# Linear attention and a gated FFN on one core: the seven-product projection starts one chunk earlier

## The chip, the core and the metric

The kernel is one program on one core of a Trainium2 chip. The metric is device time in microseconds; lower is better. The core has five instruction streams: TensorE (PE in the profile, with its weight loads as PEld), VectorE (DVE), ScalarE (ACT), GpSimd (POOL) and SyncE (SP), which here only issues transfers.

## The reference

Inputs are q, k and v of shape 8 x 8 x 576 x 64 (batch, heads, sequence, head width), two 512 x 1536 weights and one 1536 x 512 weight, all fp32.

```python
q_s = softmax(q, axis=-1)              # over the 64 features of a head
k_s = softmax(k, axis=2)               # over the 576 positions
kv  = einsum('bhsd,bhse->bhde', k_s, v)
x   = einsum('bhsd,bhde->bhse', q_s, kv)   # then laid out as 4608 tokens x 512
out = ((x @ w_a) * (x @ w_b)) @ w_out      # "gate", then "projection"
```

## The kernel before, in words

**Tiling.** The 4608 tokens are worked in nine chunks of 512, numbered c = 0 to 8. The 1536 hidden features are six pairs n = 0 to 5 of 256. Every matrix product is made at nearly fp32 accuracy out of three products of split numbers: each operand is kept as a rounded high part and the rest (`split`, L593: a copy on ACT gives the high part, a subtraction on DVE at L599 the low part), and high by high, high by low and low by high are added up in PSUM.

**Gate.** Chunk 0 takes the gate products plainly, while the weights are still being converted (the startup). From chunk 1 on each pair of x @ w_a and x @ w_b is a 2 x 2 block product made with seven block products in place of eight (L1127, 84 matmuls of 256 columns for a pair, 504 for a chunk). The seven x operands of the next chunk, B11, T2, T3, T1, B21, T4 and B22, are made at the end of a chunk by `x_operands` (L1055); four of them need subtractions, 128 x 512 each (L1071, L1072, L1077, L1082). These run on DVE, or on POOL when `lean` is set, which it is from the chunk before `SEVEN` on. The seven weight operands of a pair, 512 KB each, are read anew from memory for every chunk (`get_w`, L728 to L730), into eight buffers `ws`, or seven from chunk `SEVEN - 1` on (`few`, L1914).

**Projection.** Up to chunk `SEVEN - 1` it is the plain product (`project`, L1147): 12 feature blocks by 4 token blocks by 3 split products by 2 halves of 256 columns, 288 matmuls for a chunk (L1017, `po`). From chunk `SEVEN` on (4 before) it is made of seven block products too (`seven`, L1832): two halves by six pairs by 7 products by 3, 252 matmuls of the same 256 columns (L1847, `pp`). It needs more operands. The weight side is made once, pair by pair, in `seven_operands` (L1768): six instructions on POOL (L1774, L1779) and four splits for each of six pairs, at the places of the list `seven_places` (L1889): two pairs in chunk `SEVEN - 1`, four in chunk `SEVEN`, put into tiles that nothing uses any more by then. The activation side is made in `prepare` (L1790) for each half of each pair: four subtractions on POOL (L1817) and two splits. Its inputs are the gated features, whose four multiplications per pair are shared by DVE and POOL (`quarter`, L2002) from chunk `SEVEN` on, and are all on DVE before (L2022 to L2040, tile `cc`). `bring_out` (L1856) adds up the seven products of a half, four instructions on DVE and one on ACT, where the plain form has a copy on ACT.

**Attention.** The x of chunk c + 1 is worked out while chunk c multiplies (`attention_tasks`, L1250), from `SEVEN` on in another form. Keys up to there go through `key_steps` (L1178): maxima with three DVE instructions for each of four head groups, a reduction over the partitions on POOL (L767), a subtraction on DVE (L799). Later keys go through `keys_late` (L1201): a transposed copy of the keys is loaded (`ktt`), DVE takes the maximum of each row (L1212), TensorE transposes it (L949), it goes out to memory and back to all partitions (`dk`, `mk`), and POOL subtracts (L1234). The query addition (`q_exp`, L993) is on DVE before `SEVEN` and on POOL from it on (both L994). Chunk 3 has buffers of its own (`roomy`, L963).

**Order.** The order of work is written out: `ORDER` holds, for PE, DVE, ACT, POOL and SP, the list of all instructions by name, one step after the other, and `arrange` (L1655) chains each engine's instructions in that order. An item such as `pair.11*12` stands for the next 12 gate matmuls of step 11, where step numbers are 6(c - 1) + n; `proj`, `step` and `attend` are projection, the rest of a step, and attention. Each engine works through its list in that order, and what stands behind a waiting instruction waits too. The lists interleave gate, projection and attention matmuls closely, so that one product's wait is covered by another's matmuls.

```python
SEVEN = 4
(nc.gpsimd if c >= SEVEN else nc.vector).tensor_tensor(out=qt, in0=qt, in1=rows[0], op=ALU.add)
run_pending() if pend else seven()
```

Of the kernel before, what the change touches and what calls it, by code (L numbers as in the profile page):

```python
# [31 lines left out]
        "tr0*5 warm*25 tr1*5 pq0*4 pk0*10 pk1*10 tr3*4 tr2:4 pq1*4 tr3 tr2*4 px0 pk3*9 px1 pk3 pk2*10 pq2*4 "  # L32
        "pq3*4 g00*2 g00:10*8 g00*6 g00:4*4 px3 px2 g10:12*4 g10*20 g00*4 g01:12*3 g01*19 g11:12*4 g11*16 "
        "g01*2 g11*4 g20*12 g21*12 p0:2*2 p0*6 g20*12 g21*12 turn.0*3 proj.1:4 turn.0*2 proj.1:4 proj.1*2 "
        "proj.2*2 gate.3*48 proj.2:2*2 proj.1 proj.1:1 proj.1*2 proj.2:2*2 prod.0*10 gate.4*6 gate.4:18*24 "
        "proj.3:12*2 turn.1*4 proj.3:16*2 gate.4*18 proj.3*4 proj.3:12*2 proj.3:8*2 gate.5*12 proj.2*2 turn.1 "
        "gate.5:12*4 gate.5*2 proj.3:10*2 proj.3:2*6 gate.5:10*12 gate.5*6 gate.5:4*8 gate.5*3 proj.3:2*2 "
        "gate.5 turn.2*3 prod.1*10 turn.2 proj.4:6*2 proj.4:16*2 gate.6*11 gate.6:13*9 proj.3*2 proj.4*2 "
        "gate.6:13*3 gate.6*18 turn.3*4 gate.6*7 proj.4*8 proj.4:6*2 proj.4*8 proj.5:18*2 proj.5:12 "
        "proj.5:6*2 prod.2 turn.4*3 gate.7*10 proj.5:10*2 gate.7:14*4 proj.5:10 gate.7:14*2 proj.5 gate.7*2 "  # L40
        "proj.5*2 gate.7:12*4 prod.2 turn.4 gate.7:12*2 proj.5:9*4 proj.5 gate.7:12 gate.7*5 gate.7:7 "
        "proj.5:6*2 gate.7*2 proj.5:2*2 proj.5*2 turn.3 gate.7*3 gate.7:2*5 gate.7*5 proj.6*2 proj.6:16*2 "
        "proj.5*2 proj.6:4*2 proj.6:8*2 turn.5*4 prod.3*10 gate.7 proj.6:12*2 proj.6*2 proj.6:2*2 gate.7 "
        "proj.6*2 proj.6:2*6 gate.8*20 gate.8:4*7 proj.6*2 gate.8:4*7 gate.8*12 proj.7:12*2 proj.7:6*2 "
        "proj.7*2 proj.7:8*2 gate.8*2 proj.7:10*4 prod.4*2 turn.6*4 proj.7:8*2 proj.7:4*4 proj.7*4 turn.5 "
        "gate.9*11 gate.9:13*20 prod.5*10 proj.7*2 proj.8:18*2 proj.8*2 gate.9*13 proj.8:10*2 proj.8*2 "
        "proj.8:12*2 gate.9*4 proj.8:8*2 turn.7*3 gate.10*10 turn.7 prod.6*2 gate.10:14*12 proj.8:10*2 "
        "proj.8:2*2 gate.10*2 proj.8:2*2 proj.8:4*2 proj.8:2*2 gate.10:12*4 gate.10*8 gate.10:4*8 turn.8 "
        "gate.10*4 prod.7*2 proj.8*2 proj.9:6*2 proj.9*2 proj.9:8*2 proj.9*2 proj.9:10*2 prod.8 proj.9:2*2 "
        "proj.9:8*2 gate.11*15 gate.11:9*12 gate.11*9 proj.9:4*2 gate.11*4 proj.9:2*2 gate.11*4 proj.9*4 "  # L50
        "pair.0*9 proj.10*2 proj.9*2 gate.11*4 proj.10:10 proj.10:4*2 proj.10:8 pair.0 pair.0:14*6 pair.0*2 "
        "pair.0:12*2 pair.0*4 attend.0*10 pair.0:8 pair.0*9 proj.10:12*2 proj.10*2 pair.0 pair.0:13*3 "
        "proj.10:6*2 pair.0:13*3 proj.10:8*2 pair.0:13*3 pair.0:1*4 pair.0:9 pair.0:1*3 pair.0:6 pair.0:1*4 "
        "pair.0:2 pair.0 proj.10:6*2 pair.0 proj.0:12*2 proj.10*4 proj.0*2 proj.10*2 proj.0:4*4 proj.10*2 "
        "proj.0:10*4 pair.0:12*8 proj.0:10*2 pair.0*4 pair.0:8*4 pair.1 pair.0 proj.0*4 proj.0:2*2 pair.0 "
        "pair.1 pair.0 pair.1*3 proj.0:2*2 pair.0*5 proj.0*2 pair.1 pair.1:18*2 pair.1*5 pair.1:1 pair.1*5 "
        "pair.1:7*4 pair.1 attend.1 pair.1:6*2 pair.1*4 pair.1:2 pair.1:17*5 proj.1*2 pair.1*2 proj.1*2 "
        "pair.1*2 proj.1:14*2 pair.1:13*2 proj.1:2*2 pair.1 proj.1:12*2 pair.1:12*3 pair.1*10 proj.1:12 "
        "pair.1 proj.1:12 proj.1:2*2 pair.1:1 pair.1*2 proj.1:2*2 pair.1:12*5 proj.1:26*2 pair.1:12*5 "
        "proj.1:2*2 pair.1*4 attend.1 pair.1:8*2 pair.1*6 proj.1:12*2 proj.1:22*2 pair.2*4 proj.1:2*2 pair.1 "  # L60
        "pair.2 proj.1:10*2 pair.1 proj.1:18*2 pair.2 proj.1*2 proj.1:2*2 proj.1*2 pair.2:18*3 pair.2 "
        "pair.2:17*2 pair.2 pair.2:4*2 proj.1:6*2 attend.1 pair.2:14*3 pair.2*2 pair.2:2*3 pair.2:9 pair.2:2 "
        "pair.2 proj.1*2 pair.2:1 pair.2*3 proj.1:4*2 pair.2 proj.1:4*2 proj.1:2*2 pair.2*2 proj.1*2 "
        "proj.2:6*2 proj.2*2 proj.2:14*4 pair.2:3*4 pair.2 proj.2*2 pair.2:2*3 proj.2:2*2 pair.2:7*7 "
        "pair.2:2*4 pair.2*2 pair.2:1*4 pair.2 proj.2*2 pair.2 proj.2:10*2 attend.1*10 pair.2:12*5 pair.2*3 "
        "pair.2:9 pair.2*3 pair.2:6*2 pair.2*6 proj.2:8*2 proj.2:2*2 pair.2*2 proj.2:22*2 pair.2*2 proj.2:2*2 "
        "proj.2*2 proj.2:6*2 pair.3:12*2 pair.3*7 attend.1 pair.3 proj.2*2 proj.2:14*2 pair.3*3 proj.2*2 "
        "pair.3 proj.2:12*2 pair.3*4 pair.3:6*2 proj.3:18*4 pair.3:6 pair.3*3 pair.3:3*2 proj.2:6*4 pair.3*3 "
        "proj.3:18*2 pair.3 proj.2:6*2 proj.2*2 proj.3:12*2 pair.3:18*4 pair.3:6*3 pair.3 proj.2*2 attend.1 "
        "pair.3:14*3 pair.3:5 pair.3:13 proj.2*2 pair.3:13*2 attend.1 pair.3:13 pair.3 pair.3:4 pair.3 "  # L70
        "pair.3:3*2 proj.3:34*2 pair.3:3 pair.3 proj.3:12*2 proj.3:6*2 pair.3:2 proj.3:10*2 pair.3*2 "
        "attend.1*10 pair.3 pair.3:2 proj.3:28*2 proj.3*2 pair.3*2 proj.3:4*4 proj.3*2 pair.3:12*7 proj.3*2 "
        "pair.3:12*3 pair.3 pair.4 pair.3*2 pair.4 pair.3*2 pair.3:7 proj.3:6*2 pair.3:7 pair.4*2 proj.3:6*2 "
        "attend.2 pair.3 proj.3*2 pair.4 pair.3*3 proj.3*2 proj.3:4*2 pair.4 pair.3*3 pair.4:18*2 proj.3:8*2 "
        "proj.3*4 pair.4:18 pair.4*2 pair.4:4*4 pair.4*2 pair.4:10 pair.4 attend.2*10 pair.4:1*3 pair.4 "
        "pair.4:5*2 pair.4*2 pair.4:3 pair.4*2 proj.3*2 proj.4*2 proj.4:16*2 pair.4 proj.4*2 pair.4*2 "
        "proj.4:2*2 proj.3*2 proj.4:12*2 proj.4:6*2 pair.4 proj.4:6*2 pair.4 proj.4:2*2 pair.4:1 pair.4*3 "
        "attend.3 pair.4*2 proj.4*2 attend.3*2 proj.4*2 pair.4 pair.4:6*2 pair.4*4 attend.3 pair.4 attend.3 "
        "pair.4:1*6 proj.4:2*2 pair.4 pair.4:16*2 pair.4*2 attend.3 proj.4:20*2 proj.4*2 pair.4 pair.4:13*3 "
        "pair.4 pair.4:12*2 proj.4:12*2 proj.4:6*2 pair.4:12*3 proj.4:14*2 pair.4*7 proj.4:10*2 pair.4 "  # L80
        "proj.4*2 pair.4*3 pair.4:1*2 pair.5*2 attend.4 pair.5*2 pair.4 proj.4*2 pair.5 attend.4*3 pair.5:19 "
        "pair.5 pair.5:18*2 pair.5 attend.4 proj.4:2*2 pair.5:5 proj.4*2 pair.5 pair.5:4 pair.5*3 attend.4 "
        "pair.5:11 proj.4:2*2 pair.5:1 proj.4*2 pair.5:10 pair.5:1*2 pair.5:8 proj.5:6*4 pair.5:1 proj.4*2 "
        "pair.5:7 pair.5*2 proj.5:8*2 pair.5 pair.5:4 proj.5:6*2 pair.5:4 pair.5 pair.5:3 proj.5:10*2 "
        "proj.5*2 pair.5*2 proj.5*2 attend.4 pair.5 pair.5:14*2 attend.4 pair.5*2 attend.4*2 pair.5:12*3 "
        "attend.4*2 pair.5*5 proj.5:2*2 pair.5:7*2 proj.5:14*2 pair.5 proj.5:4*2 pair.5:6 pair.5*3 proj.5*2 "
        "pair.5*2 proj.5:2*2 pair.5*5 proj.5*2 proj.5:6*2 proj.5:8*2 pair.5*6 proj.5:8*2 pair.5 pair.6 "
        "proj.5:10*4 pair.5*2 attend.4 pair.5 pair.6 pair.5 proj.5*2 pair.6*2 pair.5 attend.4*2 proj.5*4 "
        "attend.4*2 pair.6 attend.4 pair.6 proj.5*2 pair.5*8 proj.6:6*2 pair.5*4 pair.6*4 proj.5:2*2 "
        "proj.6:16*2 pair.6:2 pair.6 proj.6*2 proj.6:14*2 pair.6 proj.6:4*2 pair.6*7 proj.5*2 proj.6:6*2 "  # L90
        "pair.6 proj.6:4*2 pair.6 pair.6:2 pair.6*2 proj.6:4*2 pair.6:23 proj.6:6*2 pair.6:23*3 proj.6:12*2 "
        "proj.6*2 proj.6:2*2 pair.6*8 pair.6:15 proj.6*2 pair.6 pair.6:2*3 pair.6:11*2 pair.6:2*2 pair.6*3 "
        "pair.6:6 proj.6:10*2 pair.6*2 proj.6:6*2 pair.6*4 pair.6:16 proj.6:12*2 pair.6 proj.6:8*2 "
        "proj.6:10*2 proj.6:6*2 proj.6*2 pair.6*3 pair.6:12*3 pair.6*5 pair.6:7*3 proj.6:6*2 pair.6 pair.7*2 "
        "pair.6*2 pair.7*2 pair.6*2 pair.6:2 pair.7 pair.6:2*2 pair.6 pair.6:1 proj.6*2 pair.7 proj.6:2*2 "
        "pair.6:1 pair.6 attend.6*20 pair.7 pair.7:5 pair.7 proj.6*2 pair.7:4*3 pair.7*2 pair.7:2*3 pair.7 "
# [2005 lines left out]
```

## Time and profile before

| what | value |
|---|---|
| time, median of 3 runs | 947.04 us (946.09 to 949.88) |
| time of the profiled execution | 951.79 us |
| its span, first to last instruction | 949.8 us |
| TensorE busy in it | 904.1 us, 95% |
| DVE, ACT, POOL busy | 688.7, 423.0, 383.6 us |
| transfers | 259.26 MB, mean 273 GB/s |

The profiled execution is one run; 2.0 us of its time lie outside the span. The kernel's source lines are those of the listing above. Helpers record many operations under one line (L599 is every low part of a split, L1127 every gate matmul), so the tile written and read tells them apart: `gl<-cc` is the split of the gated features, `xo<-xf` that of an x operand, `ws<-dw` a weight read.

Chunks do not show in the profile by name. Their borders are found by counting along TensorE's list in `ORDER`, since its matmuls run in that order: the first gate matmul of chunks 1 to 6 starts at 143.1, 251.6, 362.8, 466.1, 551.3 and 649.6 us, that of chunk 7 at 748.7 us.

### The profile page before, as it was taken

To read this page: it belongs to the slowest core of one execution; us is meant where nothing else is said; L and a number is where in the kernel's file an instruction comes from. 1 tells how busy PE (TensorE), PEld (TensorE's weight loads), DVE (VectorE), ACT (ScalarE), POOL (GpSimd) and SP (SyncE) were. 2 spreads that over 40 slices of the span, in tenths; PEclk is the share of its full clock that TensorE was granted. 3 is DMA by queue.
4 is the path that set the end of the run, shared out by engine and by line. 5 is a ranking of instruction groups with operands and counts; after the bars stand their busy time and mean duration, and the time that the engine had idled before them with its cause. 6 is when DMAs were issued, how large, how long until landed. Compare 5 with 4: busy or idle time off the path is not lost.

```text
span 949.8 us, 21010 instructions
## 1 busy us (share of the span) xinstructions
PE 904.1 (95%) x7973; PEld 880.3 (93%) x7973; DVE 688.7 (73%) x1197; ACT 423.0 (45%) x1170; POOL 383.6 (40%) x464
## 2 busy tenths in 40 slices
PE   7999987999999989999999999999999999999997
PEld 6888987999999989998989999999999999999997
DVE  7999898887875486755877596768666756774555
ACT  8877874533552233522553346234532452332122
POOL 1554443232010070413285465463635633662434
PEclk9999999999999999999999999999999999999999
DMA  9787957998999974999599988995999289838851
GB/s 345 299 312 271 374 209 262 324 321 271 299 338 275 304 261 146 321 285 311 184 307 328 330 294 308 312 336 176 328 285 342 93 300 288 315 104 278 273 167 45
DMA packets 93027, 259.26 MB, mean 273 GB/s; under 512 B 11184, under 2 KB 13312, under 8 KB 92928
## 3 DMA queue, kind: packets, MB, share of 16 engines
q1 hardware_dynamic: 92928, 257.94, 80.6%
q8 instruction: 63, 1.03, 0.5%
q14 instruction: 36, 0.29, 0.1%
HBM read 218.86 MB, written 36.94 MB: 269 GB/s over the span
## 4 chain that ended last, share of the span: by engine, by line
PE 58%; DVE 19%; DMA 12%; issue 4%; ACT 3%; POOL 3%; SPq 1%; DVEq 0%; POOLq 0%; ACTq 0%
PE pp L1847 11%; PE kp L1127 11%; PE ka L1127 9%; PE kx L1127 9%; PE po L1017 8%; DMA ws<-dw 6%; PE ky L1127 5%; DVE gl L599 3%; DVE xo L599 2%; DMA dw<-ws 2%; PE pk L837 2%; DVE room_wy L630 2%; DMA mr<-dq 1%; PE px L1045 1%; DVE ws L599 1%
## 5 line engine op out<-in xcount | busy, mean ns | idle before, releaser
L1127 PE MATMUL ka<-xo,ws 128*128 128x256 f32 x1152 | 169.7, 280 | 7.6 <-DVE xo L599 2.3
L1127 PE MATMUL kx<-xo,ws 128*128 128x256 f32 x1152 | 170.8, 279 | 1.7 <-DVE xo L599 1.0
L1127 PE MATMUL kp<-xo,ws 128*128 128x256 f32 x1152 | 165.2, 280 | 7.2 <-DVE u L1980 3.9
L1127 PEld LDWEIGHTS ka<-xo,ws 128*128 128x128 f32 x1152 | 148.9, 189 | 9.3 <-DVE xo L599 2.5
L1127 PEld LDWEIGHTS kp<-xo,ws 128*128 128x128 f32 x1152 | 146.6, 188 | 9.9 <-DVE u L1980 5.0
L1127 PEld LDWEIGHTS kx<-xo,ws 128*128 128x128 f32 x1152 | 149.6, 188 | 2.6 <-DVE xo L599 1.2
L1017 PE MATMUL po<-wo_w,gh 128*128 128x256 f32 x720 | 121.1, 279 | 0.0
L1017 PEld LDWEIGHTS po<-wo_w,gh 128*128 128x128 f32 x720 | 100.6, 189 | 0.2
L1127 PE MATMUL ky<-xo,ws 128*128 128x256 f32 x576 | 84.3, 280 | 3.7 <-DMA ws<-dw 3.1
L930 ACT ACTIVATE qt<-qt,st 128x64 f32<-128x64 f32 x224 | 75.6, 340 | 24.9 <-DVE st L927 24.9
L1017 PE MATMUL pt<-xo,ws 128*128 128x256 f32 x576 | 77.4, 284 | 5.8 <-DVE ws L599 2.3
L1127 PEld LDWEIGHTS ky<-xo,ws 128*128 128x128 f32 x576 | 74.4, 189 | 4.8 <-DVE qtt L994 1.4
L1017 PEld LDWEIGHTS pt<-xo,ws 128*128 128x128 f32 x576 | 70.4, 188 | 9.1 <-DVE ws L599 2.8
L1847 PE MATMUL pp<-wo_w,gh 128*128 128x256 f32 x392 | 73.4, 279 | 0.3 <-ACT gh L596 0.2
L1017 PE MATMUL po<-wo_w,gl 128*128 128x256 f32 x360 | 68.7, 283 | 2.0 <-DVE gl L599 2.0
L748 POOL TENSOR_TENSOR room_wy<-room_wy 128x512 f32<-128x512 f32 x24 | 34.0, 1421 | 68.2 <-DMA room_wy<-dy 57.3
L1817 POOL TENSOR_TENSOR s<-room_wy 128x128 f32<-128x128 f32 x64 | 35.0, 550 | 64.2 <-DVE gl L599 37.5
L1847 PEld LDWEIGHTS pp<-wo_w,gh 128*128 128x128 f32 x392 | 58.9, 188 | 0.7 <-ACT gh L596 0.7
L627 POOL TENSOR_TENSOR room_wr<-raw,room_wr 128x512 int32<-128x512 int32 x24 | 36.3, 1517 | 56.0 <-DVE raw L624 40.2
L1980 DVE TENSOR_TENSOR u<-ky,u 128x512 f32<-128x512 f32 x48 | 32.9, 685 | 35.2 <-PE ky L1127 20.9
L1847 PE MATMUL pp<-wt,gh 128*128 128x256 f32 x294 | 56.2, 281 | 0.5 <-ACT gh L596 0.5
L1017 PEld LDWEIGHTS po<-wo_w,gl 128*128 128x128 f32 x360 | 53.7, 190 | 3.1 <-DVE gl L599 2.6
(216 smaller groups left out, 1907.5 us busy)
## 6 DMA issues: line engine op xcount, KB each, us to landing
ws<-dw SPq DMA_DIRECT2D x260, 512.0 KB, 6.4
dw<-ws SPq DMA_DIRECT2D x42, 512.0 KB, 6.3
raw<-in_w_ab SPq DMA_DIRECT2D x24, 512.0 KB, 7.9
mr<-dq SPq DMA_DIRECT2D x96, 128.0 KB, 6.8
out<-room_wr SPq DMA_DIRECT2D x36, 256.0 KB, 5.5
vt<-in_v SPq DMA_DIRECT2D x28, 325.0 KB, 5.2
qt<-in_q SPq DMA_DIRECT2D x32, 256.0 KB, 5.3
kt<-in_k SPq DMA_DIRECT2D x24, 320.0 KB, 5.2
```

The lines of the kernel that those rows point to most:

```text
L599: return nc.vector.tensor_tensor(out=lo, in0=src, in1=hi.bitcast(F32), op=ALU.subtract)
L627: nc.gpsimd.tensor_tensor(out=r, in0=u, in1=r, op=ALU.add)
L630: nc.vector.scalar_tensor_tensor(out=yi, in0=yi, scalar=-(2 ** 31), in1=r, op0=ALU.bitwise_and, op1=ALU.bitwise_or)
L748: nc.gpsimd.tensor_tensor(out=a[o], in0=a[x], in1=a[y], op=op)
L837: nc.tensor.matmul(pk[h * D:(h + 1) * D], kt[:, j, h], vt[:, j, h], start=(j == 0), stop=(j == J - 1),)
L930: nc.scalar.activation(out=qt[:, j, h], in_=qt[:, j, h], func=AF.Exp, bias=st[:, h, 0, j:j + 1], accum_out=st[:, h, 1, j:j + 1],)
L1017: ins = nc.tensor.matmul(out[:, n * H:(n + 1) * H], w, x[:, n * H:(n + 1) * H], start=start and n == 0, stop=stop, skip_group_check=True,)
L1045: nc.tensor.matmul(px[:, s], w, m[:, s], start=(i == 0), stop=(i == 2))
L1127: ins = nc.tensor.matmul(pt[:, n], w[:, n, wp, c], x[:, xp, c], start=(first and n == 0 and i == 0), stop=(i == 5), skip_group_check=True,)
L1817: nc.gpsimd.tensor_tensor(out=t[:, o], in0=a, in1=b, op=op)
L1847: nc.tensor.matmul(pp[bank][:, place], parts[x][:, o], w[b][y], start=(n == 0 and place == 0 and k == 0), stop=(n == NI - 1 and k == 2), s ...
L1980: nc.vector.tensor_tensor(out=u2, in0=ky, in1=u2, op=ALU.add)
```

## The change

`SEVEN` goes from 4 to 3. With it move: chunk 3's projection (seven block products, not the plain form), the two and four sets of weight operands (chunks 2 and 3, not 3 and 4), `lean` x operands for chunk 3, the seven instead of eight `ws` buffers in chunk 2, the POOL form of chunk 3's query addition, `keys_late` for the keys that chunk 3 brings in (batch 3), and chunk 3's gated features in the shared form. `roomy` holds for no chunk any more. Since odd chunks take the pairs in falling order, the list of places now goes by position and not by pair number. The input holds transposed keys from batch 3 on.

All five lists are new from the first instruction on: the startup and every other chunk, too, run in another order. Their lengths, in instructions:

| engine | before | after |
|---|---|---|
| PE | 7588 | 7553 |
| DVE | 1197 | 1186 |
| ACT | 897 | 907 |
| POOL | 456 | 524 |
| SP | 702 | 710 |

```diff
 ORDER = {
     "PE": (
...
@@ -507,7 +489,7 @@
     NCH = NT // T
     LATE = NCH - qt_late.shape[0]
     ODD = 16
-    SEVEN = 4
+    SEVEN = 3
 
     const = ctx.enter_context(tc.tile_pool(name="const", bufs=1))
@@ -1886,13 +1868,14 @@
+    p = pairs_of(SEVEN)
     seven_places = [
         (SEVEN - 1, 1, lambda: homes("mr.0") + homes("mr.1")),
         (SEVEN - 1, 2, lambda: odd_homes("ws.7") + one_home("xt.0") + one_home("xt.1")),
-        (SEVEN, 0, lambda: [room("cc.0", n) for n in range(3)] + b12_home(2)),
-        (SEVEN, 0, lambda: [room("cc.0", 3)] + [room("xo.8", n) for n in range(2)] + b12_home(3)),
-        (SEVEN, 1, lambda: [room("xo.9", n) for n in range(2)] + [room("xo.10", 0)] + b12_home(4)),
-        (SEVEN, 1, lambda: [room("xo.10", 1)] + b12_home(0) + b12_home(1) + b12_home(5)),
+        (SEVEN, 0, lambda: [room("cc.0", n) for n in range(3)] + b12_home(p[2])),
+        (SEVEN, 0, lambda: [room("cc.0", 3)] + [room("xo.8", n) for n in range(2)] + b12_home(p[3])),
+        (SEVEN, 1, lambda: [room("xo.9", n) for n in range(2)] + [room("xo.10", 0)] + b12_home(p[4])),
+        (SEVEN, 1, lambda: [room("xo.10", 1)] + b12_home(p[0]) + b12_home(p[1]) + b12_home(p[5])),
     ]
@@ -1972,7 +1955,7 @@
             for m, (at_c, at_n, places) in enumerate(seven_places):
                 if (c, n) == (at_c, at_n):
-                    seven_operands(m, places(), m % 2 * 4 * T if c < SEVEN else 4 * T)
+                    seven_operands(p[m], places(), m % 2 * 4 * T if c < SEVEN else 4 * T)
@@ -2069,7 +2052,7 @@
-    klate = k[4:].reshape(b - 4, g, 2, s, d).transpose(0, 1, 2, 4, 3).reshape(b - 4, g, P, s)
+    klate = k[3:].reshape(b - 3, g, 2, s, d).transpose(0, 1, 2, 4, 3).reshape(b - 3, g, P, s)
```

In the new POOL list the first two sets of weight operands (`step.7`, `step.8`) stand right behind the last weight sums of chunk 1 (`step.4`), three of their instructions even before the last of them; in the list of before (`step.13`, `step.14`) they stand behind the partition reductions of chunk 2 (`attend.7`).

794 rows, old and new, of the table ORDER are left out of this document.

## The prediction

> **What bounds the kernel now.** I read the page first (busy times and the chain), then the busy times by chunk, then what TensorE waited for, then the stretch with the longest wait.
>
> The page: span, busy time by engine, and the chain that ended last.
>
> ```profile
> span 949.8 us, 21010 instructions
> PE 904.1 (95%) x7973; PEld 880.3 (93%) x7973; DVE 688.7 (73%) x1197; ACT 423.0 (45%) x1170; POOL 383.6 (40%) x464
> ...
> PE 58%; DVE 19%; DMA 12%; issue 4%; ACT 3%; POOL 3%; SPq 1%; DVEq 0%; POOLq 0%; ACTq 0%
> ```
>
> TensorE sets the time, but a third of the chain runs over others, so the order counts. Busy time by stretch (length; busy time and instructions for PE, PEld, DVE, ACT, POOL; granted clock; DMA share and GB/s): the startup, chunks 1 to 6, a dense stretch of chunk 8, then four short ones.
>
> ```profile
> 0.00:143.10 143.10, 129.02 (x1095) 119.24 (x1095) 129.65 (x217) 113.60 (x277) 58.78 (x47) 1.00 0.81 300
> 143.10:251.60 108.50, 99.74 (x874) 96.70 (x875) 90.18 (x165) 44.04 (x118) 30.79 (x22) 0.98 0.87 292
> 251.60:362.80 111.20, 104.54 (x927) 102.40 (x926) 76.44 (x142) 40.84 (x123) 20.54 (x18) 0.98 0.88 283
> 362.80:466.10 103.30, 99.71 (x912) 97.87 (x911) 68.75 (x126) 39.27 (x122) 24.19 (x18) 1.00 0.83 271
> 466.10:551.30 85.20, 82.68 (x754) 80.79 (x753) 60.73 (x106) 39.22 (x118) 49.84 (x57) 1.00 0.93 311
> 551.30:649.60 98.30, 96.68 (x876) 95.14 (x875) 72.34 (x124) 40.97 (x122) 54.90 (x76) 1.00 0.86 288
> 649.60:748.70 99.10, 96.00 (x865) 94.05 (x865) 66.72 (x119) 38.53 (x118) 52.46 (x74) 1.00 0.82 269
> 850.00:900.00 50.00, 50.00 (x439) 49.96 (x438) 27.77 (x46) 10.41 (x23) 19.57 (x39) 1.00 0.79 264
> 237.00:252.00 15.00, 15.00 (x130) 15.00 (x129) 12.53 (x24) 5.50 (x11) 1.38 (x1) 1.00 0.84 258
> 343.00:358.00 15.00, 11.48 (x94) 11.08 (x93) 14.13 (x16) 6.26 (x15) 9.62 (x8) 0.99 0.59 200
> 449.00:464.00 15.00, 14.32 (x121) 13.72 (x120) 14.10 (x22) 5.72 (x16) 4.01 (x3) 1.00 0.66 227
> 357.60:361.01 3.41, 3.41 (x18) 3.41 (x18) 2.47 (x6) 0.00 (x0) 0.00 (x0) 0.50 0.00 0
> ```
>
> Length less PE's busy time is its idle time: 14.1 us in the startup, then 8.8, 6.7, 3.6, 2.5, 1.6 and 3.1 in chunks 1 to 6. In the dense stretch there is none, and 439 matmuls less about two that began before it give 50 / 437 = 114 ns a matmul. Chunk 2 has the most idle time of the chunks that the change rewrites, over half of it at its end, 343 to 358 us, where PE idles 3.5 us and DVE is busy for 14.13 of 15. There, on PE, DVE and POOL (start, length, what; in brackets the idle time before it):
>
> ```profile
> 350.06 0.74 PE L1017 MATMUL po<-wo_w,gl 128*128 128x256 f32 x4 [1.16 <-DVE gl L599]
> ...
> 356.50 0.74 PE L1127 MATMUL kp<-xo,ws 128*128 128x256 f32 x4 [2.36 <-DVE u L1980]
> ```
>
> ```profile
> 344.83 0.68 DVE L2039 TENSOR_TENSOR cc<-ka,u 128x512 f32<-128x512 f32 x1
> 345.43 1.41 DVE L1072 TENSOR_TENSOR xt<-xf,xt 128x512 f32<-128x512 f32 x1
> 346.25 4.34 POOL L1779 TENSOR_TENSOR room_wy<-room_wy 128x256 f32<-128x256 f32 x4
> 348.80 2.35 DVE L599 TENSOR_TENSOR gl<-cc,gh 128x512 fp32r<-128x512 f32 x2
> ```
>
> The end of chunk 2 does two jobs at once: DVE makes chunk 3's x operands, subtractions and splits, while POOL makes the first weight operands of the projection. DVE instructions with two inputs in SBUF take up to twice the 0.68 us that one reading PSUM takes. Two results that PE needs come late, and then the granted clock is 0.50 for 3.41 us, in which 18 matmuls start where 3.41 / 0.114 = 30 would: 12 x 0.114 = 1.4 us lost.
>
> **The change part by part.** The sum is made against the profiled execution's own 951.79 us (span 949.8 and 2.0 around it), 4.75 above the median of 947.04; I take the difference off the median.
>
> *Matmuls.* Chunk 3's projection falls from 288 to 252, all of 256 columns: 36 x 0.114 = **-4.1 us**. PE is busy for 96 to 98% of these chunks, so I count all of it (bounds -4.1 and, if the time saved all turned into waiting, 0).
>
> *Keys and queries of chunk 3.* Rows of the groups involved, in their forms before and after (mean ns behind the busy time):
>
> ```profile
> L949 PE MATMUL pst<-ident,st 128*4 128x128 f32 x4 | 1.1, 270 | 0.0
> L767 POOL PARTITION_ALL_REDUCE mx<-m x4 | 3.6, 922 | 40.5 <-DVE m L778 40.5
> L799 DVE TENSOR_TENSOR kt<-kt,mx 128x640 f32<-128x640 f32 x4 | 3.2, 814 | 0.0
> L994 POOL TENSOR_TENSOR qtt<-qtt,mr 128x512 f32<-128x512 f32 x20 | 27.8, 1390 | 57.6 <-DMA mr<-dq 39.4 <-DVE xf L1296 10.6 <-DMA qtt<-in_q_late 4.0
> L1234 POOL TENSOR_TENSOR kt<-kt,mk 128x640 f32<-128x640 f32 x16 | 25.7, 1613 | 42.9 <-DMA ws<-dw 29.7 <-DMA kt<-in_k 9.5 <-PE ky L1127 1.8
> L1212 DVE TENSOR_REDUCE st<-ktt 128x1 f32<-128x576 f32 x16 | 11.6, 741 | 0.0
> ```
>
> PE gets one transposition (**+0.1**; at most its whole 0.27). Four partition reductions leave POOL (3.6 us), and eight additions come, 4 x 1.39 + 4 x 1.61 = 12 us, beside 111 us in which POOL works 20.5. DVE loses the subtractions (3.2 us) and gets four reductions (3.0). Neither is on PE's path unless late; a wait of POOL for `mk` delays the x of chunk 3 alone, needed a chunk later.
>
> *Chunk 3's projection inputs.* 60 more POOL instructions (12 multiplications, 48 subtractions) make chunk 3 like chunk 4 is now: POOL 49.8 us instead of 24.2, in 85 us. Chunk 4 idles 2.5 us and chunk 3 3.6, chunk 5 1.6 and chunk 4 2.5: if each takes on the row of the next, **-2.0** over both; I take half, **-1.0**, since the keys differ (bounds -2.0 and +2).
>
> *The end of chunk 2.* The four x subtractions move to POOL and the weight operands are already made: what chunk 3's end is now, where the same lean form idles 15 - 14.32 = 0.7 us in its 15 us against 3.5. I take **-2.4**, leaving 0.4 for a second small wait (bounds -3.5 and 0). Without a wait of this length there is no half clock: **-1.4** (bounds -1.4 and 0).
>
> *Two sets of weight operands at the end of chunk 1.* 12 POOL instructions and eight splits now stand where DVE makes chunk 2's x operands, in the 15 us around 237 to 252, where PE now never idles and DVE has 2.5 us to spare. The nearest row for the same collision is the 3.5 us at the end of chunk 2. I take **+2.0** (bounds 0 and 3.5, and 1.4 more if the clock falls too), between the two because DVE has more room here.
>
> The Trainium skill has a rule that speaks against this: GPSIMD Engine Reference, Key points, says that GpSimd shares its SBUF interfaces with VectorE and contends with DVE instructions that have two SBUF inputs. The trace agrees: the 1.41 and 2 x 1.18 us above, under POOL's 4.34. It makes the moved collision one of the rivals.
>
> *Transfers.* Chunk 2 gets four transposed key blocks and the maxima's round trip, and one weight buffer fewer.
>
> ```profile
> ktt<-in_k_late SPq DMA_DIRECT2D x4, 288.0 KB, 9.4
> room_wy<-dq SPq DMA_DIRECT2D x16, 128.0 KB, 7.8
> ```
>
> 4 x 0.295 + 0.26 (two blocks like the second row's) = 1.4 MB at chunk 2's 283 GB/s, 5 us of transfer time. SP issues eight more, queued among the weight reads that PE needs. Chunk 2's DMA share is 0.88, so it fits; I take **+1.0** (bounds 0 and 5).
>
> *The lists.* Every engine's order is new. Chunks 5 and 6 do the same work and idle 1.6 and 3.1 us: a spread of 1.5 for a chunk, over nine stretches 1.5 x 3 = 4.5. One chunk that came out as chunk 1 does now instead of as chunk 5 would cost 8.8 - 1.6 = 7. I take **0**, bounds -4.5 and +7.
>
> Sum: -4.1 + 0.1 - 1.0 - 2.4 - 1.4 + 2.0 + 1.0 = -5.8, about -6: 946 for a run like the profiled one, **941 us** at the median.
>
> **The rivals.**
>
> *The collision only moves.* The wait at the end of chunk 2 comes back at the end of chunk 1, whole, and with the half clock: 3.5 + 1.4 for 2.0, +2.9 on the sum, 944 us. For it: the new POOL list puts the weight operands there. Against it: DVE's 2.5 us to spare, and PE's 15.00.
>
> On the clock, the Trainium skill (TensorE: Matmul & The Clock Gate, Why this matters for your kernels) says no idle gap over about 3 us. Here 1.16 and 2.36 us within 8 us were enough, so by the trace the 1.4 us would come with the moved wait; by the rule they would not, and this rival would be at 943 in place of 944.
>
> *Transfers run out (the other side).* Chunk 3 shrinks by up to 18 us, from 103.3 to chunk 4's 85.2, with its transfers unchanged. DMA-busy time now is 0.88 x 111.2 + 0.83 x 103.3 = 183.6 us in chunks 2 and 3; with 5 more 188.6, in 111 - 5 + 85 = 191: a share of 0.985. The long stretches above reach 0.93 at most. At 0.93 the two chunks take 203, 12 us more than forecast: 953 us. Slower than now from a share of 188.6 / 197 = 0.96 down. Against it: the seven buffers of 512 KB are 3.7 MB, 12 us at 311 GB/s, that can be read ahead, and chunk 4 at 0.93 idles only 2.5 us.
>
> *The lists decide.* Startup and chunk 1, which hold 22.9 us of idle time and nothing of the change, come out 4.5 us better or 7 us worse: 936.5 or 948.
>
> That the change does not do what it says I leave out: the list of PE is 35 shorter.
>
> **How the numbers follow.** Forecast 0.50, moved collision 0.24, transfers 0.12, lists better 0.07 and worse 0.07. A difference of 0.5% (4.7 us) is about what a measurement tells from none: faster is below 942.3, slower above 951.8. Faster: 0.43 of the forecast's 0.50 (its own range is 937 to 945), 0.05 of the collision, 0.07 of the lists: 0.55. Slower: 0.10 of the transfers, 0.01 of the collision and 0.01 of the worse lists: 0.12. Same: the rest, 0.33. The range is 934 (all bounds of gain at the end of chunk 2 with better lists) to 950 (worse lists, or transfers at a share of 0.945); beyond it lie the worst 0.10 of the transfers and some 0.05 at the fast end.
>
> **What would show it.** PE matmuls fall by 35 and L1017 `po` by 288, L1847 `pp` grows by 252. At the end of chunk 2 no PE wait above 1 us, and granted clock 1.00 there. At the end of chunk 1 a PE wait on a DVE split or `u`, with POOL L1779 above it: under 2 us for the forecast, 3.5 for the rival. DMA share in chunk 3 of 0.95 or more with PE waits on `ws<-dw` under 2 us in all; above 5, the transfers decide. PE idle of startup and chunk 1 within 4.5 of 22.9. The forecast is wrong if the time stays above 945 or if the gain comes from the startup.

## The result and the profile after

| | before | after |
|---|---|---|
| time, median of 4 runs each on one chip | 946.57 us (945.44 to 949.88) | **903.93 us** (899.82 to 905.43) |
| ratio, 95% interval | | **0.954** (0.950 to 0.958) |
| span of the profiled execution | 949.8 us | 901.9 us |

The change made the kernel 42.6 us faster. The forecast was 941 us, a gain of 6, and its range ended at 934: the sign was right, the size wrong by a factor of seven. The two profiled executions lie 47.9 us apart, because the one of before was 5 us above its median; numbers by stretch contain these 5 us, and those of other kernels a like difference where their profiled run is off the median.

Lines up to about L1870 stand 18 lower in the kernel after: the gate matmuls are L1109, the low part of a split is L581, the plain projection L999, the one of seven products L1829.

The page of the kernel after: span, busy time by engine, and the chain that ended last.

```profile
span 901.9 us, 21088 instructions
PE 882.2 (98%) x7938; PEld 868.1 (96%) x7938; DVE 655.1 (73%) x1186; ACT 426.4 (47%) x1180; POOL 428.1 (47%) x532
...
PE 89%; DMA 5%; DVE 2%; POOL 2%; issue 1%; ACT 1%; SPq 0%; POOLq 0%; DVEq 0%; ACTq 0%
```

The chain tells most: PE's share of it goes from 58% to 89%, and DVE's from 19% to 2%. The span splits in three. PE's idle time falls from 949.8 - 904.1 = 45.7 us to 901.9 - 882.2 = 19.7, by 26.0. The 35 matmuls fewer give 35 x 0.114 = 4.0. But PE's *busy* time falls by 21.9, 17.9 more than these 35 explain: the same matmuls are recorded as shorter. The ends of matmuls are modelled, and a matmul whose successor comes a little late fills the time between; at most 2.8 of it were the two half clocks of before (1.4 us each). So some 15 us of what the old profile shows as busy was not work of the matmuls. The starts bear this out: time over 114 ns from one matmul's start to the next's, where the profile counts no idle time, adds up to 54.5 us before and 36.2 after, 18.2 less. That these were short waits for operands is the likely reading; no run shows it one by one. The Trainium skill says this of the view I used (Perfetto Trace Analysis, Identifying the Most-Contended Engine): busy time of pipelined matmuls is no good measure of how near TensorE is to its limit. The 17.9 us agree that it is none, though the reason given there, that pipelined instructions look smaller, is another.

Busy times by stretch of the kernel after: the startup, chunks 1 to 8, then the ends of chunks 1 and 2 (columns as in the prediction; borders counted along PE's new list).

```profile
0.00:136.00 136.00, 126.65 (x1101) 119.88 (x1102) 115.76 (x220) 113.50 (x280) 62.47 (x48) 1.00 0.89 326
136.00:234.70 98.70, 98.14 (x897) 96.87 (x895) 84.31 (x167) 46.06 (x125) 37.77 (x28) 1.00 0.96 331
234.70:337.60 102.90, 99.42 (x911) 97.69 (x910) 77.09 (x136) 47.07 (x155) 30.19 (x25) 1.00 0.89 302
337.60:421.30 83.70, 82.61 (x768) 81.45 (x768) 61.78 (x110) 36.01 (x102) 52.24 (x61) 1.00 0.95 323
421.30:513.30 92.00, 92.00 (x846) 90.99 (x845) 64.35 (x118) 40.04 (x120) 51.59 (x72) 1.00 0.90 300
513.30:609.60 96.30, 95.99 (x884) 95.22 (x883) 69.93 (x125) 42.49 (x126) 54.06 (x76) 1.00 0.92 300
609.60:704.10 94.50, 94.50 (x863) 93.56 (x862) 66.83 (x120) 44.26 (x149) 49.18 (x70) 1.00 0.82 274
704.10:793.60 89.50, 89.50 (x785) 89.50 (x784) 55.93 (x95) 29.28 (x70) 46.38 (x73) 1.00 0.79 254
793.60:901.90 108.30, 103.37 (x904) 102.93 (x903) 59.11 (x102) 27.72 (x57) 44.19 (x84) 0.99 0.54 190
220.00:235.00 15.00, 15.00 (x131) 15.00 (x130) 13.80 (x22) 7.84 (x22) 5.55 (x5) 1.00 1.00 346
323.00:338.00 15.00, 14.24 (x125) 13.90 (x124) 12.19 (x22) 8.26 (x32) 2.58 (x2) 1.00 0.67 221
```

For the two stretches of before that the prediction did not show, chunks 7 and 8:

```profile
748.70:839.50 90.80, 90.61 (x783) 90.21 (x782) 63.28 (x103) 39.52 (x120) 43.86 (x67) 1.00 0.77 256
839.50:949.80 110.30, 105.10 (x905) 103.89 (x903) 60.62 (x102) 27.05 (x55) 48.20 (x89) 0.99 0.56 187
```

| stretch | before, us | after, us | shorter by |
|---|---|---|---|
| startup (work unchanged) | 143.1 | 136.0 | 7.1 |
| chunk 1 (two sets of operands more) | 108.5 | 98.7 | 9.8 |
| chunks 2 to 4 (rewritten) | 299.7 | 278.6 | 21.1 |
| chunks 5 to 8 (work unchanged) | 398.5 | 388.6 | 9.9 |

(Chunks 5 to 8 are 98.3 + 99.1 + 90.8 + 110.3 before and 96.3 + 94.5 + 89.5 + 108.3 after. Between neighbouring chunks a few dozen matmuls change sides of a border, so single chunks compare less well than these groups.) Startup and chunks 5 to 8, where the form of the projection is the same in both, are 17.0 us shorter, far more than the 5 us by which the profiled run of before was long. The form of these stretches has no part in them.

What PE waited for over the whole run, after:

```profile
PE pka L1465 <- ACT kt_first L1459: 9.4, 1, 9.4
PE pst L931 <- DVE kv L862: 0.9, 1, 0.9
PE po L999 <- ACT gh L578: 0.9, 1, 0.9
PE ky L1109 <- DMA ws<-dw: 0.9, 1, 0.9
...
PE kx L1109 <- DMA ws<-dw: 0.6, 1, 0.6
```

Besides the first 9.4 us, before any operand is there, no wait reaches 1 us.

### The profile page after: what moved, and what is told of

Its sections match the earlier page's. It is cut to its first block, busy times and chain, and to the rows that moved or that the text cites. A ratio compares the mean times of both kernels' runs of the same rounds, so it can differ in the third digit from the quotient of the medians.

```text
span 901.9 us, 21088 instructions
## 1 busy us (share of the span) xinstructions
PE 882.2 (98%) x7938; PEld 868.1 (96%) x7938; DVE 655.1 (73%) x1186; ACT 426.4 (47%) x1180; POOL 428.1 (47%) x532
## 4 chain that ended last, share of the span: by engine, by line
PE 89%; DMA 5%; DVE 2%; POOL 2%; issue 1%; ACT 1%; SPq 0%; POOLq 0%; DVEq 0%; ACTq 0%
PE pp L1829 18%; PE kx L1109 13%; PE kp L1109 13%; PE ka L1109 13%; PE po L999 10%; PE pt L999 7%; PE ky L1109 6%; PE pk L819 2%; DMA ws<-dw 2%; DMA mr<-dq 2%; PE px L1027 2%; PE px L1012 1%; PE warm L537 1%; DMA kt<-in_k 1%; DMA qts<-in_q 1%
## 5 line engine op out<-in xcount | busy, mean ns | idle before, releaser
L1109 PE MATMUL kx<-xo,ws 128*128 128x256 f32 x1152 | 155.1, 278 | 1.5 <-DMA ws<-dw 0.6
L1109 PE MATMUL ka<-xo,ws 128*128 128x256 f32 x1152 | 155.9, 277 | 0.2 <-DMA ws<-dw 0.2
L1109 PE MATMUL kp<-xo,ws 128*128 128x256 f32 x1152 | 153.3, 278 | 0.3 <-DVE u L1966 0.3
L1109 PEld LDWEIGHTS kx<-xo,ws 128*128 128x128 f32 x1152 | 141.9, 188 | 2.4 <-issue 0.8
L1109 PEld LDWEIGHTS ka<-xo,ws 128*128 128x128 f32 x1152 | 142.5, 188 | 0.5 <-DVE gl L581 0.4
L1109 PEld LDWEIGHTS kp<-xo,ws 128*128 128x128 f32 x1152 | 141.2, 188 | 0.7 <-PE kx L1109 0.4
L1829 PE MATMUL pp<-wo_w,gh 128*128 128x256 f32 x488 | 91.8, 278 | 0.0
L999 PE MATMUL po<-wo_w,gh 128*128 128x256 f32 x528 | 87.8, 281 | 0.9 <-ACT gh L578 0.9
L1109 PE MATMUL ky<-xo,ws 128*128 128x256 f32 x576 | 76.3, 278 | 0.9 <-DMA ws<-dw 0.9
L999 PEld LDWEIGHTS po<-wo_w,gh 128*128 128x128 f32 x528 | 72.3, 188 | 1.9 <-ACT gh L578 1.1
L999 PE MATMUL pt<-xo,ws 128*128 128x256 f32 x576 | 74.1, 283 | 0.0
L1829 PEld LDWEIGHTS pp<-wo_w,gh 128*128 128x128 f32 x488 | 73.5, 188 | 0.3
L1109 PEld LDWEIGHTS ky<-xo,ws 128*128 128x128 f32 x576 | 70.3, 188 | 1.3 <-issue 1.0
L999 PEld LDWEIGHTS pt<-xo,ws 128*128 128x128 f32 x576 | 69.3, 188 | 2.3 <-issue 1.9
L1829 PE MATMUL pp<-wt,gh 128*128 128x256 f32 x366 | 70.0, 279 | 0.0
L578 ACT CAST gh<-room_wy 128x384 fp32r<-128x384 f32 x61 | 31.1, 510 | 76.4 <-PE pp L1829 63.1
L1829 PE MATMUL pp<-wo_w,gl 128*128 128x256 f32 x244 | 65.6, 279 | 0.0
L1799 POOL TENSOR_TENSOR room_wr<-room_wy 128x128 f32<-128x128 f32 x68 | 38.4, 570 | 52.5 <-DVE gl L581 33.9
```

Source lines behind the costliest of these rows:

```text
L578: nc.scalar.copy(out=hi, in_=src)
L999: ins = nc.tensor.matmul(out[:, n * H:(n + 1) * H], w, x[:, n * H:(n + 1) * H], start=start and n == 0, stop=stop, skip_group_check=True,)
L1109: ins = nc.tensor.matmul(pt[:, n], w[:, n, wp, c], x[:, xp, c], start=(first and n == 0 and i == 0), stop=(i == 5), skip_group_check=True,)
L1799: nc.gpsimd.tensor_tensor(out=t[:, o], in0=a, in1=b, op=op)
L1829: nc.tensor.matmul(pp[bank][:, place], parts[x][:, o], w[b][y], start=(n == 0 and place == 0 and k == 0), stop=(n == NI - 1 and k == 2), s ...
```

## The experiments

The lists can be exchanged apart from the form, which gives two theories. **Form**: the gain comes from where the projection's work now lies. **Lists**: it comes from the new order of everything, and the form is worth about its matmuls. In the kernels below a list is the head of one order, cut at a time of its trace, followed by all the rest in the other order. Their lines stand up to some 15 off those of the kernel that they are made from.

### The new order's head in the old form, and the reverse

`s4_new_start`: `SEVEN = 4`; all five lists begin as the new ones do (startup and nearly all of chunk 1).

```diff
     "PE": (
-        "tr0*5 warm*25 tr1*5 pq0*4 pk0*10 pk1*10 tr3*4 ...
+        "tr0*4 warm*8 tr0 tr1*4 warm*9 tr1 warm*6 pk0*10 pq0*4 ...
```

> The kernel before (seven products from the fifth chunk on), with the new lists' order for everything that the changed kernel had started in its first 221 us (startup and nearly all of chunk 1), and the old order for all the rest. Theory 'lists': the startup and chunk 1 hold the same work in both kernels and took 251.6 us before and 234.7 after, so the new order alone takes 17 us off, less a few at the joint: 930 us (926 to 936). Theory 'form': the gain comes from the earlier seven-product form and what it frees; with the form of before the new order gives nothing here: 945 to 949 us.

Measured: 927.34 us (922.96 to 933.03) beside 947.16, ratio 0.980 (0.974 to 0.985), within what the lists were expected to give. Startup 134.9 us, and the half clock at the head of chunk 1, which before has at 149.4 us, is gone. 20 us came without any of the change's form.

`s4_new_ends`: the same edit, and behind all that the kernel before has begun by 563 us (early in chunk 5) the rest follows in the order of the new lists. PE's tail, for instance:

```diff
-        "pair.45*36 proj.45*21 pair.45:12*7 pair.45*29 step.45:105*11 ...
+        "pair.44*12 step.44:105*5 step.44:106*6 step.44:105*7 pair.45*36 proj.45*21 pair.45*36 step.45:105*11 ...
```

> As the run with the new order in startup and chunk 1, and from 563 us of the old order on (chunk 5's first steps) the rest in the new order too; chunks 2 to 4 stay in the old order, form of before. Chunks 5 to 8 took 398.5 us before and 388.6 after. Theory 'lists': 947 - 17 - 10 = 920 us (915 to 927). Theory 'form': 945 to 949 us.

Measured: 928.53 us (927.64 to 936.49), ratio 0.982 (0.977 to 0.988): no more than the head alone, not the 920 expected. At the joint PE waits 10.1 us once, and the granted clock is 0.50 for 10.24 us there: that eats what the order gains behind it. Behind the joint the stretches are as short as after.

```profile
PE pp L1839 <- ACT gh L588: 10.2, 2, 10.1
```

Chunks 6, 7 and 8 took 94.9, 89.4 and 109.0 us, against 99.1, 90.8 and 110.3 with the old lists and 94.5, 89.5 and 108.3 with the new: 6.9 us of the 7.9 come in the old form too.

`s3_old_start`: `SEVEN = 3`, with the old order for the first 237 us.

```diff
     "PE": (
-        "tr0*4 warm*8 tr0 tr1*4 warm*9 tr1 warm*6 pk0*10 pq0*4 ...
+        "tr0*5 warm*25 tr1*5 pq0*4 pk0*10 pk1*10 tr3*4 ...
```

> The changed kernel, with the old order for everything that the kernel before had started in its first 237 us (startup and most of chunk 1), the new order for the rest. Theory 'lists': the 17 us come back: 921 us (915 to 926), with the half clock near 150 us again. Theory 'form': 902 to 907 us.

Measured: 925.82 us (924.39 to 929.37), ratio 0.978 (0.974 to 0.982). The startup takes 143.1 us, as before, and chunk 1 111.8, longer than the 108.5 of before, with the half clock at 149.35 us back. About half of the gain, 20 to 22 us, sits in startup and chunk 1 and goes with the order in both forms.

### Both forms without any list

`s4_free` and `s3_free` chain nothing; the framework that compiles the kernel orders each engine by itself.

```diff
-    for engine, names in ORDER.items():
+    for engine, names in ():
```

> The kernel before with none of the five lists applied: each engine's order is the one that the building framework makes from the program, by one rule for this and its partner run (seven products from the fourth chunk, no lists). It only serves the comparison of the two. Slower than the kernel before by an amount that no theory states: 960 to 1150 us.

> The changed kernel with none of the five lists applied, beside its partner run. Theory 'lists': with the order made by one rule for both, the earlier seven-product form is worth its 36 matmuls and a little of waiting: 3 to 10 us less than the partner. Theory 'form': the form itself is worth most of the 43 us: 25 us or more less than the partner.

Measured, 10 runs each: 951.91 us (947.49 to 959.34), ratio 1.005 (1.002 to 1.009), and 948.36 us (944.82 to 953.75), ratio 1.000 (0.998 to 1.003). The first lies below the 960 to 1150 expected. Two things follow. Without lists the two forms are 951.91 - 948.36 = 3.6 us apart, about the 4.1 of the 36 matmuls. (Not all of it need be theirs: the framework's order differs between the two as well, and their startups take 162.5 and 159.7 us.) And the old lists were worth 3.0 us over none (948.91 against 951.91), the new ones 948.36 - 903.93 = 44.4 (across two chips, whose medians of before are 2.3 apart).

The 3.0 us hide two large differences. In the profiled runs without lists and with the old ones, the startup takes 162.5 against 143.1 us, and the rest 787.2 against 806.7. (31 more matmuls, 3.5 us, lie ahead of the border without lists.) So the old lists gained some 16 to 19 us in the startup and lost as much in chunks 1 to 8, where they were worse than the framework's own order.

### The matmuls given back

`s3_more36`: the kernel after with 36 extra matmuls in chunk 3's projection.

```diff
+                if c == SEVEN and k == 2 and place == 0 and bank < 3:
+                    nc.tensor.matmul(pp[bank][:, place], parts[x][:, o], w[b][y], ...)
```

> The kernel after, with the 36 matmuls of 256 columns given back that the seven products save in chunk 3: the low-by-high term of three of the products is made twice, each copy right behind the matmul that it repeats (what is summed differs by that term, so the output is not quite the reference's). Everything else and every list stand as in the kernel after. If every matmul of chunk 3 lies on the path, as the prediction counted: 36 x 0.114 = +4.1 us, 908 us (907 to 909.5), chunk 3 at 87.7 us in place of 83.6. If chunk 3 of the new lists is held by transfers or by VectorE, the extra matmuls fill PE's idle time: 904 to 905.5.

Measured: 906.70 us (903.69 to 911.33), ratio 0.958 (0.954 to 0.962); profiled span 904.0 against 901.9. The 36 matmuls cost 2.1 us by the spans, 2.8 by the medians and 3.8 by the ratios, each to the kernel before on its own chip. The median lies between the two expectations, and the intervals overlap: inconclusive by itself. With the pair without lists it leaves the term of the matmuls at 2 to 4 us.

### Which list does it

`s3_oldsp`: the kernel after, only SP's list old for the first 143 us. `s3_oldnosp`: the reverse, the other four old and SP's new.

```diff
     "SP": (
-        "lq0 eye lq1 lk0 lk1 lq3 lw00 lk3 lq2 lk2 lv0 lv1 lw10 ...
+        "lq0 lk0 eye lk1 lq1 lq2 lw00 lk2 lq3 lv1 lk3 lv0 lo2 ...
```

> The changed kernel, with the old order in SP's list alone (the transfers that the kernel before had issued in its first 143 us come first, in the old order); the four other lists are the new ones. If the startup's 7 us lie in the order of transfers: 909 to 913 us. If they lie in the order on the computing engines (DVE and POOL out of each other's way): 903 to 906 us.

> The changed kernel with the old order of the first 143 us in the four computing engines' lists, and the new list for SP. The converse of the run with SP's old list alone, which took 918 us with a startup of 147 us. If the transfers' order holds the startup's gain: startup 135 to 138 us and 902 to 908 us in all. If it takes both: startup 140 us or more, 908 to 915 us.

Measured: 917.70 us (916.72 to 918.89), ratio 0.969 (0.965 to 0.973), startup 147.1; and 927.33 us (924.64 to 930.74), ratio 0.978, startup 152.4. Both startups are longer than either kernel's own, 143.1 and 136.0. The times, too, lie above both ranges that were expected of each. So neither reading (SP's order alone, or the others' alone) fits, and the lists work only together. With SP's old list the trace shows how:

```profile
SPq L883 <- PE pq L990: 25.9, 4, 11.5
```

SP stands 25.9 us, 11.5 at a time, at loads of q whose buffers PE frees later in the new order, and everything queued behind waits too.

`s4_qload`: the kernel before with three such entries of SP put back a few places, since SP stood 9.2 us at one of them.

```diff
-        "raw.8:2 raw.7 b.5 raw.7 load.6 out.5 wl21 a.6 raw.8 b.3 raw.8 load.5 ...
+        "raw.8:2 raw.7 b.5 raw.7 out.5 wl21 a.6 raw.8 b.3 raw.8 load.6 load.5 ...
```

> The kernel before with three entries of SP's list moved and nothing else: the three query loads of the startup that wait on SP longest (9.2, 5.0 and 6.4 us, until their buffer is free), each put behind the two to six transfers that stood behind it. If head-of-line waiting on SP is what delays the startup's weight loads: startup 137 to 140 us in place of 143, 941 to 944 us. If single waits do not matter: 945 to 949 us.

Measured: 947.19 us (940.20 to 955.47, 10 runs), ratio 0.997 (0.993 to 1.001), startup 143.3. No effect, though SP's waits at the loads of q in the startup fell from 25.3 to 5.2 us: it stood longer at writes that need DVE's joins instead, 38.4 us in place of 24.2. So the waits at the loads of q are not what made the old startup long.

### VectorE behind POOL

What does differ between the startups is how long the same DVE instructions take. The line that joins the two halves of a weight word, before and then after, for the 32 instructions that write `room_wy` (four more write `yo`). The weights are not fp32, as the section on the reference has them: the kernel reads them as 64-bit words (`int64`, L2082), and five instructions make fp32 of a tile of them: two on ACT (L620, L621), a shift on DVE (L624), an addition on POOL (L627) and the join on DVE (L630).

```profile
L630 DVE SCALAR_TENSOR_TENSOR room_wy<-room_wy,room_wr 128x512 int32<-128x512 int32 x32 | 31.7, 997 | 0.0
```

```profile
L612 DVE SCALAR_TENSOR_TENSOR room_wy<-room_wy,room_wr 128x512 int32<-128x512 int32 x32 | 24.6, 779 | 0.2 <-POOL room_wr L609 0.2
```

One by one the times fall in two groups: 22 of the 32 before take 0.68 us and ten take 1.38 to 1.78. Six are long after, four of them under 1.3. Here is where they come from, in the timeline of before (start, length): DVE first, then POOL.

```profile
90.44 1.79 DVE L599 TENSOR_TENSOR ws<-room_wy,ws 128x512 fp32r<-128x512 f32 x1
92.15 1.78 DVE L630 SCALAR_TENSOR_TENSOR room_wy<-room_wy,room_wr 128x512 int32<-128x512 int32 x1
...
97.64 0.68 DVE L630 SCALAR_TENSOR_TENSOR room_wy<-room_wy,room_wr 128x512 int32<-128x512 int32 x1
```

```profile
90.06 1.62 POOL L627 TENSOR_TENSOR room_wr<-raw,room_wr 128x512 int32<-128x512 int32 x1 [8.52 <-ACT qt L911]
91.64 1.74 POOL L627 TENSOR_TENSOR room_wr<-wo_raw,room_wr 128x512 int32<-128x512 int32 x1
...
97.80 1.67 POOL L627 TENSOR_TENSOR room_wr<-wo_raw,room_wr 128x512 int32<-128x512 int32 x1 [2.17 <-DVE wo_raw L624]
```

A join that starts inside an addition of POOL ends about 0.55 us after that addition has ended (92.15 + 1.78 = 93.93; 91.64 + 1.74 = 93.38). One that starts before POOL's (97.64 against 97.80) keeps its 0.68, and then the addition takes longer: 1.67 us, where undisturbed ones take 1.27 to 1.29. All 36 joins of this startup follow the rule: the 14 that start inside an operation of POOL are long, the other 22 are not. So the price, and who pays it, is set by which of the two starts first, that is, by the lists. Three runs test whether this made the old startup long.

`s3_pool36`: the kernel after with more POOL work of no use in the startup.

```diff
             nc.gpsimd.tensor_tensor(out=r, in0=u, in1=r, op=ALU.add)
+            nc.gpsimd.tensor_tensor(
+                out=top2[:, 0:DM // 2], in0=top2[:, 0:DM // 2], in1=top2[:, 0:DM // 2], op=ALU.add
+            )
```

> The kernel after, with one more addition on POOL (128x256, int32, in place on bits that nothing reads any more) behind each of the 36 additions that join the two halves of a weight word in the startup; nothing else is moved. By its size about 0.75 us each, 27 us of POOL beside its 64 us in the 136 us of the startup. If DVE's lengthening under POOL is what made the old startup slow (DVE's instructions took 31 us longer than their shortest there, 15 us in the kernel after), DVE's share of that goes back towards 25 to 30 us and the startup to 142 to 148 us: 910 to 916 us. If POOL's idle time takes them and the gain came from which work is ready when, the startup stays within 2 us of 136.0: 904 to 906 us.

Measured: 913.73 us (911.33 to 914.09), ratio 0.964 (0.960 to 0.968), startup 144.2: within the expectation of lengthening, outside that of idle time. The joins are as slow as before the change:

```profile
L622 DVE SCALAR_TENSOR_TENSOR room_wy<-room_wy,room_wr 128x512 int32<-128x512 int32 x32 | 31.9, 1006 | 0.1
```

`s4_halfadd` and `s3_halfadd`: POOL's additions over half the columns, in the old and in the new kernel. The low bits of the other columns are left out, so these weights are off in their last digits.

```diff
-            nc.gpsimd.tensor_tensor(out=r, in0=u, in1=r, op=ALU.add)
+            nc.gpsimd.tensor_tensor(
+                out=r[:, 0:DM // 2], in0=u[:, 0:DM // 2], in1=r[:, 0:DM // 2], op=ALU.add
+            )
```

> The kernel before with its own lists. Each of the 36 additions on POOL that join the two halves of a weight word in the startup covers 256 of its 512 columns (the low bits of the other columns are left as they come from ACT, so these weights are off in their last digits). POOL loses about 27 of its 60 us in the startup; no instruction is moved. If the old startup was long because DVE's instructions wait behind POOL's (ten of the 32 joins at L630 took 1.38 to 1.78 us, the others 0.68), their mean of 997 ns falls below 850, DVE's busy time in the startup by 8 us or more, and the startup from 143.1 to 134 to 138 us: 938 to 943 us. If the startup hangs on which work is ready when (loads, SP's order), it stays at 141 to 143 us whatever POOL does: 945 to 948 us.

> The same edit in the kernel after with its new lists (the low bits of half of the weight columns left as they come from ACT). There six of the 32 joins took 0.86 to 1.58 us. If DVE's wait behind POOL is what still costs in this startup, it falls from 136.0 to 131 to 134 us and the time to 898 to 902 us. If the new lists have it off the path already, 135 to 137 us and 903 to 905 us.

Measured: the old kernel falls to 937.68 us (932.48 to 940.73), ratio 0.990 (0.986 to 0.994), its startup from 143.1 to 132.1, both a little below what the collision was expected to give; the new one stays at 904.30 (902.60 to 907.51), ratio 0.955 (0.951 to 0.958), startup 135.9. The startups in rows: old lists with half additions, new lists with half additions, new lists with more POOL work.

```profile
0.00:132.10 132.10, 125.59 (x1095) 118.42 (x1096) 111.26 (x218) 113.49 (x277) 40.24 (x47) 1.00 0.87 325
```

```profile
0.00:135.90 135.90, 126.62 (x1102) 119.84 (x1103) 106.82 (x220) 113.39 (x280) 42.10 (x48) 1.00 0.89 326
```

```profile
0.00:144.20 144.20, 130.74 (x1102) 120.64 (x1103) 133.98 (x220) 114.52 (x280) 93.61 (x83) 1.00 0.83 304
```

| startup | POOL busy, us | DVE busy, us | length, us |
|---|---|---|---|
| old lists | 58.8 | 129.7 | 143.1 |
| old lists, half additions | 40.2 | 111.3 | 132.1 |
| new lists | 62.5 | 115.8 | 136.0 |
| new lists, half additions | 42.1 | 106.8 | 135.9 |
| new lists, more additions | 93.6 | 134.0 | 144.2 |
| new lists, SP's old (`s3_oldsp`) | 62.4 | 115.4 | 147.1 |

The new lists have more POOL work in the startup than the old (62.5 against 58.8) and yet 13.9 us less DVE time. By the first five rows DVE sets the length of the startup where it is busy for 130 us; from 116 down it does not, since another 8.9 us less change nothing. The last row shows that DVE is not the only thing that can: with SP's old list the startup is 11.1 us longer than with the new one at the same DVE time. And with half the additions the *old* startup is the shorter of the two, 132.1 against 135.9: the old lists were not the worse ones in themselves, they met POOL more often. The half addition also makes each join ready earlier, which the run cannot tell from the shorter wait behind POOL; the added work behind the addition makes no join ready earlier, and says the same. Its own flaw is small: the added work holds a buffer longer, and SP waits for it 2.4 us once.

## Why the prediction was wrong, and where it was right

**The step that failed is the lists: "I take 0, bounds -4.5 and +7".** With both forms freed of lists, the old lists are worth 3.0 us and the new ones 44. (The old lists' 3.0 are themselves a gain and a loss of 16 to 19 us, as seen above.) The bound was taken from the spread of PE's idle time between two chunks of *one* set of lists. That shows how evenly those lists came out, and nothing of what a better set could do. It was also taken from PE's idle time, which left out some 15 us inside PE's busy time that were no work. The page of before had the room in plain sight: 42% of its chain ran over something else than PE, and the prediction called it "a third", read it as "the order counts" and then gave the order a term of nothing. Its rival "the lists decide" had the right mechanism and place (startup and chunk 1 do change by 17 us), with 4.5 us as its end. The prediction's own sign of being wrong is there, too: PE's idle time in startup and chunk 1 is 9.4 + 0.6 = 9.9 us, 13 below the 22.9 that it allowed to move by 4.5.

**What bounds the kernel.** "TensorE sets the time" held for the chunks, and not for the startup: there DVE was busy for 129.65 of 143.10 us, a row that the prediction quoted and then used for its idle PE alone. It even quoted DVE instructions of 1.41 us under POOL's and cited the Trainium skill for it (GPSIMD Engine Reference, Key points), and looked for this collision only where the form moved it, not where 47 instructions of POOL ran anyway. Two of its readings there are off. The operation that held up the 1.41 us at 345.43 us is not the row shown, which starts later, but the one ahead of it, 1.30 us from 345.00. And two inputs in SBUF do not make a DVE instruction long by themselves: the like subtraction at 343.11 us, clear of POOL, took 0.68, and the one at 351.07, inside an operation of POOL, 1.78, more than the "up to twice" of the prediction.

**The matmuls, -4.1.** Right within 2: the pair without lists gives 3.6, the 36 given back 2.1 to 3.8.

**The end of chunk 2, -2.4, and the half clock, -1.4.** Right as seen: 15.00 - 14.24 = 0.8 us idle there, no wait above 0.9, clock 1.00. But PE's idle time fell in every chunk, also where the form moved nothing, so this may be luck: no run shows that the moved work did it. And the half clock is not a fixed price: with the same lists in chunk 2, `s4_qload` and `s4_halfadd` show none at its end.

**Two sets of operands at the end of chunk 1, +2.0.** They cost nothing that can be seen: PE is busy for 15.00 of 15.00 us between 220 and 235 us, and chunk 1, counted from its first gate matmul to the 505th, takes 100.5 us with them and 100.6 without (`s4_new_start`). The rival that the collision only moves falls with it. POOL's timeline there (start, length, idle time before in brackets) shows why DVE has room: POOL pauses for 1.9 to 5.7 us between these operations.

```profile
217.13 1.29 POOL L1756 TENSOR_TENSOR room_wy<-wo_w 128x512 f32<-128x512 f32 x1 [2.45 <-DVE ws L581]
224.12 1.29 POOL L1756 TENSOR_TENSOR room_wy<-wo_w 128x512 f32<-128x512 f32 x1 [5.70 <-DVE ws L581]
227.32 0.74 POOL L1761 TENSOR_TENSOR room_wy<-room_wy 128x256 f32<-128x256 f32 x1 [1.92 <-ACT cc L2006]
```

**Transfers, +1.0, and the rival that they run out.** Chunk 3 reaches a share of 0.95, as the rival said, and its waits on `ws<-dw` are one of 0.9 us and one of 0.2; chunk 1 runs at 0.96 with 0.6 us idle. The ceiling of 0.93 was only the highest share that the old lists had happened to use.

**Keys and inputs of chunk 3, +0.1 and -1.0.** Not tested apart. Chunks 2 to 4 are 21.1 us shorter, of which the form has about 4 by the runs above; the rest is put down to the lists by difference, and no run splits it, since lists and form cannot be exchanged there.

**The range.** Its lower end of 934 does not follow from the parts named for it: 941.2 less 1.1 (the rest of the bound at the end of chunk 2) and 4.5 (better lists) is 935.6. It makes no difference to 904.

**What stays open.** For the startup the collision is shown as a cause of the 7 us. That the rest of chunks 1 to 8 gained by the same collision is not shown: PE's longest waits in chunk 1 of before were on DVE's results, which fits:

```profile
PE ka L1127 <- DVE xo L599: 2.3, 1, 2.3
PE kp L1127 <- DVE u L1980: 1.5, 2, 0.9
PE ka L1127 <- DVE u L1983: 1.1, 1, 1.1
```

But no run took POOL's work out of these chunks. A count over the two traces says where to look. For each DVE instruction that starts inside an operation of POOL, take the time above what its operation and shape takes undisturbed (the tenth percentile). In the startup this falls from 30.1 to 14.1 us, in chunk 1 from 16.0 to 9.3, in chunks 5 to 8 from 29.7 to 22.0, beside 7.1, 9.8 and 9.9 us that these stretches are shorter. In chunks 2 to 4 it falls only from 28.7 to 26.5, and they are 21.1 us shorter: there the collision accounts for little of it, and what does the rest stays open.

## What to carry to other kernels

When a diff replaces a written order of all work, that is a change of its own, and often the larger one: take the room for it from the share of the chain that does not run over the bounding engine (42% here, an upper end and no forecast), not from the spread within one order, and run both forms without any order to see what the form alone is worth. Look at single durations of one line and shape: two groups (0.68 us, and up to 1.78) point at a collision that a mean of 997 ns hides. An engine's busy time is no measure of its work where its records can stretch: 17.9 us of "busy" PE went away here with the same matmuls.

## What the runs showed of the hardware

A DVE instruction with two SBUF inputs that starts inside a POOL addition of two tensors waits for nearly all that is left of it (up to 1.78 us in place of 0.68), while one that starts just ahead of POOL's loses nothing and makes POOL wait (1.67 us in place of 1.28). The shift at L624, which reads one tensor, is held up the same way (all 5 that start inside an operation of POOL in the startup of before, none of 31 others); a maximum over 128x512 that starts inside one is not (0.67 us, L890 at 89.08 us after). In the startup, 31 us more of POOL work cost DVE 18.2 us (133.98 - 115.76) and the kernel 9.8 us; 18.5 us less in the old kernel gave DVE 18.4 and the kernel 8.7. And DMA shares of 0.95 and 0.96 over a whole chunk, at 323 and 331 GB/s, left PE with 1.1 and 0.6 us of idle time.
